# Retention followed by a token and channel mixer on one core: two loads of q moved to the hardware queue, a third batch in seven products, and a new order of work

## The chip, the cores and the metric

The kernel runs on one core of a Trainium2 chip. The time is the device time of one execution in microseconds (us). Before the change three runs gave 189.17, 189.81 and 190.44 us; their median is 189.81 us. One more execution was profiled, and the profile below is of that one.

The engines are named as in the profile: PE multiplies matrices, PEld loads its weights, DVE and ACT work elementwise, POOL (GpSimd) issues most of the loads here, and SP issues the stores, the transposes by DMA and one load. PSUM has eight banks, and a product lands in a bank before DVE or ACT takes it out.

## What is computed

Four batches, 8 heads, 768 tokens, 64 columns a head; x has 512 columns. The decay per head is a constant, so the kernel does the recurrence in six chunks of 128 tokens.

```python
state = gamma * state + k_t v_t^T               # per head, token by token
y_t   = (q_t state) / sqrt(64)                  # x = y, heads side by side: 4 x 768 x 512
h = relu(xT @ w_tok1) @ w_tok2                  # over tokens: 768 -> 256 -> 768
u = x + hT
out = u + relu(u @ w_ch1) @ w_ch2               # over channels: 512 -> 1536 -> 512
```

## The kernel before

**Tiling.** The work of a batch is cut in two. `front(b, p)` does the retention and the token mixing for one of four pairs of heads (128 columns): decay of k and q (L522, `decayed`), transposes of k and q by PE or by DMA (L538, `turn`), the states (L584, L596), the scores (L635) and their mask on DVE (`am`, L646), the rows of y (L666, L692), the two token products (L723, L743), and the evacuations to `x`, `u` and `X` (L708). At its end `uT`, the transposed u, is made for the pair. `back(b)` does the channel mixing of a batch: a wide product u @ w_ch1 to 1536 columns and a narrow one back to 512. Fronts of later batches run beside the backs of earlier ones.

**Two forms of the wide product.** `widen(sh)` is the direct one: for each half of the tokens and each of 12 column blocks four matmuls of 128x384 are summed in a bank (L822), and ACT takes it out with a relu (L838). `widen7()` is a product of 2x2 blocks in seven products instead of eight: four differences of `uT` on DVE (L861), then for each of six blocks seven products of two matmuls (L891), three copies of a bank kept aside (`us`, L902, ACT or DVE), three adds of bank and copy on DVE (L911), three relus on DVE (L915), and one relu straight out of a bank (L942 or L944). The combined weights that it needs are made on DVE once (L1138, tile `late`). A kept copy stands between two products in the same bank: the next product into that bank waits for it. Before the change `WIDE7` names batches 2 and 3. All four batches use the seven products in the narrow product (`narrow7`: L1005, L1041, L1051, L1031, L1058), except one part of batch 3, which is direct (`narrow`: L967, L976).

**What sets the order.** Nothing is scheduled at run time. `ORDERED` is a table of numbers of operations in the order in which they are issued, and `WAYS` picks for each the engine where two can do it. `arrange` walks the table with assumed durations and with `Rings`, a model of the DMA queues, and settles buffers and banks; the instructions are then issued in that order. Each engine works off its own list in order. Where the plan leaves PE idle in the first 21 us, matmuls on zeros are put in (L1164, tile `zero`).

**Loads.** They are issued by POOL with a cast from f32 to f16 on the way, in the order of `ORDER` as `ORDERED` places them. Only the first k (`HARD`) is loaded by SP as f32 into a buffer `us`; its decay makes f16 of it. q of batches 0 and 1 is loaded "wide": each partition takes six adjacent tokens, one run of 1536 bytes a head instead of 256. Its decay is multiplied in when the transposed q leaves its bank (L562, with the tile `late`).

Of the kernel before, what the change touches and what calls it, by code (L numbers as in the profile page):

```python
# [9 lines left out]
FP = mybir.dt.float32  # L10
# [28 lines left out]
class Rings:  # L39
# [5 lines left out]
    LAND = dict(SP=900, ACT=2000)  # L45
    DT = 40.0
    LATER = 1000
# [20 lines left out]
    def step(self, landed):  # L68
        dt, t = self.DT, self.t
        on = [(q, l[0]) for q, l in self.line.items() if l and l[0][2] <= t]  # L70
        if on:
            round_ = sum(x[0].dma[1] for _, x in on)
            for q, x in on:
                n = dt / round_
                if x[3] > t:
                    n = min(n, dt / self.GEN[q])
                x[1] -= n
                if x[1] <= 0:
                    self.line[q].pop(0)
                    landed.append((x[0], t + dt + self.land(q, x[0], t)))  # L80
        self.t = t + dt
# [9 lines left out]
def arrange(ops, BUFS, BANKS, seq, ways):  # L91
# [164 lines left out]

ORDERED = (
    "0b0d000a08050e0107020c2423040j060f292a030i2b250927260h282h2i2k0g332c2m342j0l352l37362d0k2e47382f2o2g0m43482q"
    "2n443h3i3k0n493l454a4b463m0q392p4c3a4h0o3j534d2r3b4k544e2s4i3c4f3d0p2t4j4g3e4l3f0s572u4m553g4n583n564o4p3p3o"
    "3q3r5i3s0u5l2v2y5m2w3t4r2x0v2z593u4q5a305h5b3v0t4s5c3y5d3w4t5e5j5f0w6763644u315k5g5o4v0r3z3x5n5p325q4w855r40"  # L260
    "0x4y4x86415s654z5t420z6650515u6894520y5v955y5w69115z6h5x76606j61hm1362hj6lij6ahn6k12hkim7372hp6b6ihlik106chq"
    "hsil6d77hrht74hois6e75786fithu79in7a147g7bioi4iu7jj16g7c6n7ihvhw7h6mj27ki5177d6oi77ei6iy6q1zhyhx6pi86rja21j3"
    "jgjh7f18206si9jijb6ti11c8182iv6ujciz6v6xig226yidi26w15hzi3iwi0jdihix83ia84ibj41aj01viej5iiip6z1w70j616j7icje"
    "if1yjn711987jj7m7o88iqjljo7lj81gjkir7nkb89j91xjfjp9z1b8ajukc7pjqaxjs8b1e7q8cjv8fk5jt8djy8i908gjw91k77r8hjxa0"
    "kgjm7s8ja18ek1khb0b18k7tjz8mk28l7u8njr7w1fb2k0a57x96kr8okk1d7v97ksk98pkl7y1h9892a6kaa28q93k61ukv99a78ra87z9a"
    "kwa9kea3809ba4aa8sk89cl0ay8tkt9eazkf9d8v9gkil19f8wkx9i8x9h8u9jl4kjctku9l9kky9m9n1ib3kdkn9ob4abb58ycu1sb69p8z"
    "b7kol21jb89qbvl5byadackz1ml39rag9u9sl9ae1t9vafl69wah9t9xl7bb9yaiajbfakal1nldbcamlelaanmdbdljbzmempc0mfaolfb9"
    "maapcvlkban4mqbeaqmrn5arcwbhm1bwbjasatbxllbgbiaumy1kmbn6kqavczc1mc1om2bkc2m7c3mzd0bldrmjepn0m8c4d1m3mkl8bmm9"
    "mlcxd2lyeq1lcybnmvkmlzlg1rd3bolbc5d4mwawbpbrmxlhbqm4k4dsm5k3bsc6mglibtlvm0lsd5m6c9eslmcdlwfnmhcblxlnlpcalolq"
    "ccltlrc7d7lummc8d8msd6mtcfdbmnn1etmod9njeumuminankn7ndcedtn2da1pn8nbnen9cgo5duncnfn3ddcidfcholevcjdxo6ordydv"  # L270
    "dzckdwe0glosnhewfoexe1noerclningdcnmey1qnpe2decmomnncpdgnlopcnezdhf0nqgmcqoonscrcsconrondie3ntoqfpnvf1djf2e5"
    "nwbuoufqe4e6dke8ovdnlce9dloynye7dmkpf3donzozowotdqdpf7eaebo1edeco3oxeef6p0eff4frf5ftegnuf9fup3o0nxeho4fso2f8"
    "faeip4o8p7ejp6p1fcfbgro7ekoafvo9fwfdgsocp9gtelfxodobfegup2ohffp8gooegvemoifgfyeneoofpbfhgwfjogpcpsfzfig1ptpg"
    "g4fkpdg5pxphpipepypjg2pzpkq0papufmplq1pqg0qqq2pngxpvgnq7q4flpoq9q8q5qgqrqxg3qaqvgyprqsqwqeqbqtqfqygpr7qcqzqh"
    "gqg6r0g8qir5gag7r2qjokr6g9ror3gbqlr9r8qmrercr1rppfqorardrqqdojrtpmr4rfqururrgcrgq3rwrhrvrxrmripwgdrjryqps3rn"
    "rbgerss4rzghqks0rkgfthtdgitjgjtfgktis1gggztesvh1tmh2srtoh0sws9tntph3h4tqqnssh6h5rlh7h8stt0q6h9tkt2t1tltrtss2"
    "tghattpptvtuhbt4s5hcs6t5hfhdt3sxs7hgt6s8sahihhsehet7sysbp5susgsfszsiscsht9t8sjsksdtbtzsnslsmu3uku0u4u5ulsoum"
    "u1u8upunu9uau6uqurubu2ustaucviutv8uduiuoufuuuzuguwv1vjuxvktwvnv2uvv3tyuevovlv6spvpv4v7vqtxv0vzvrv9wnvsvavxuj"
    "v5w1vbvuvywgvvvdvgvmw0vew6vhytw4w2whylwiu7w5w3wlvcuhymwjw7wmy5uyw8vwwowky6w9wpwevtwbwqwfwvvfsqwswrwcxnwwwtx1"
    "wdwuwaynxpxjxkyoxox3wxypxsxlx2wyyqxuxtxqxmxwx4x6wzxxxvx8x7xyx9yrydx0xaxzxcy0xby7x5y3y8xdysxfxetcy1xgxhy9xiy2"  # L280
    "yaxryey4yfybygyhyiycyuyvywyjyxyyykyzz0"
)
WAYS = (
    "000000000000000000000000000000000000000000000000000000000000000000000000000100000000000010000000000000100001"
    "001000000000000000000000000000000001101000000000000000000000000100100000100000000000000000000000000000000100"
    "001100000000000100000000000000011000001000000000001000000000000000000000010000000000000000000000000000000000"
    "000000000000000000000000000000000010001100000000000000000000010100000010010000000010000000000001001001011011"
    "000000010000000000100100100001100100000001100000000000000000000110110000000000000000000000000000010011000000"
    "010000000000000000100001001000000000000000000000000000000010010000000010000000000000000000000000000000000000"
    "000000000000000000000000000000000000000000000000000000000000000000000000000100000000000000000000011000000000"  # L290
    "000000000001100000000000000000000000000000000000000000000000000000000000000000000000000000000000000000000110"
    "000000000000000000001000000000000000000001100000000000000000000000000000000000000000000000000000000000001000"
    "000000000000000000000000000000000000000000000000000100000000010000000000000000000000100000000000000000000110"
    "000000000000000000000000000000000000000000000000000000000000000100000000000000000000000000000000000000000000"
    "0000000100000000011000000000000000000001000000001000000010000000100000001"
# [4 lines left out]
def kernel(  # L300
# [36 lines left out]
    WIDE7 = (2, 3,)  # L337
# [11 lines left out]
    HARD = {(0, 0, "k")}  # L349
# [129 lines left out]
    def load(b, p, what):  # L479
# [12 lines left out]
        dma = (96, 17) if hard else (16, 66) if wide else (96, 13.5)  # L492
# [6 lines left out]
    def front(b, p):  # L499
# [22 lines left out]
        def decayed(tag, src, dep, g, hard):  # L522
# [12 lines left out]
            return dst, got  # L535
        K, kl = decayed("k16", KF, kd, gk, (b, p, "k") in HARD)

# [200 lines left out]
        for j in range(2):  # L738
# [12 lines left out]
            t2 = op(one("PE", (335, 500), emit), [hr, wops["t2"], x_ops[j]], [], [H1, Y[j]])  # L751
# [50 lines left out]
    def back(b):  # L802
# [150 lines left out]
        def narrow(sh, blocks=range(HC)):  # L953
            H2, rel = H2s[sh], rels[sh]
            for i in blocks:
# [3 lines left out]
                for cols in cuts:  # L959
# [23 lines left out]
                    op(either(emit, ACT=(380, 101), SP=(450, 100)), [ad], [], [X], dma=(8, 90 * w_ // C))  # L983


        def narrow7(i0, i1):
# [95 lines left out]
            for i, d in ((i1, [o21, o22]), (i0, [o11, o12])):  # L1082
                def emit(e, i=i):
                    (nc.sync if e == "SP" else nc.scalar).dma_start(out=out[b, i * P:(i + 1) * P, :], in_=X.tile[:, i])
                op(either(emit, ACT=(380, 101), SP=(450, 100)), d, [], [X], dma=(8, 90))
# [111 lines left out]
```

## Time and profile before

| | before |
|---|---|
| median of three runs | 189.81 us |
| the profiled execution: time | 190.01 us |
| the profiled execution: span of its instructions | 188.2 us |
| granted PE clock | 0.999 |
| instructions: PE, DVE, ACT, POOL | 2109, 448, 282, 62 |
| moved by DMA | 24.92 MB |

Times inside the profile count from the start of the span; 1.8 us of the time lie outside it. A busy share is the union of an engine's instructions over the span. "x192 | 36.0, 326" in a group means 192 instructions with 36.0 us of busy time in all and 326 ns for one; where the instructions overlap, 36.0 / 192 is the smaller number and is what one costs in a row of many. The chain of waits follows the end of the program back, step by step, to what released each instruction.

### The profile page before, as it was taken

How to read it: one execution, taken by the hardware profiler on the slowest of the kernel's cores; microseconds unless marked ns; L12 is line 12 of the kernel's file. 1: busy time of each engine (PE TensorE's matmuls, PEld its weight loads, DVE VectorE, ACT ScalarE, POOL GpSimd, SP SyncE). 2: the span in 40 equal slices, each digit the busy share in tenths (PEclk: the TensorE clock that was granted, in tenths of full speed). 3: DMA queues.
4: the chain of work that ended last, by engine and by line, in shares of the span. 5: the costliest groups of instructions: out<-in, count | busy, mean ns of one | idle time of the engine just before them, and what ended most of it. 6: DMA issues, size and time to landing. Idle time of an engine off the chain costs nothing.

```text
span 188.2 us, 5284 instructions
## 1 busy us (share of the span) xinstructions
PE 181.2 (96%) x2109; PEld 136.7 (73%) x2109; DVE 166.5 (88%) x448; ACT 124.2 (66%) x282; POOL 52.8 (28%) x62
## 2 busy tenths in 40 slices
PE   7989999999999999999999899999999999999993
PEld 3455888667688988776668788965678986567872
DVE  3789999997889999958799989999999999999982
ACT  3965989569889898478663686598883444575100
POOL 7995686536440708405202200000000000000000
PEclk9999999999999999999999999999999999999999
DMA  9999999999999999999999979724312031121045
GB/s 122 155 157 196 179 188 177 208 191 201 159 155 144 125 155 122 147 136 163 195 163 127 115 99 251 158 43 86 98 56 45 0 101 56 72 98 59 0 177 215
DMA packets 91977, 24.92 MB, mean 132 GB/s; under 512 B 81968, under 2 KB 89008, under 8 KB 91952
## 3 DMA queue, kind: packets, MB, share of 16 engines
q0 software_dynamic: 67456, 13.18, 85.3%
q1 hardware_dynamic: 23776, 10.10, 24.5%
q10 hardware_dynamic: 720, 1.31, 1.9%
q8 instruction: 16, 0.26, 0.6%
q14 instruction: 9, 0.07, 0.1%
HBM read 26.74 MB, written 6.29 MB: 175 GB/s over the span
## 4 chain that ended last, share of the span: by engine, by line
PE 78%; DVE 12%; DMA 3%; ACT 2%; issue 2%; POOL 1%; SPq 0%; POOLq 0%; ACTq 0%; DVEq 0%
PE bank L822 16%; PE bank L891 15%; PE bank L1041 14%; PE bank L1051 10%; PE bank L743 5%; DVE am L646 4%; PE bank L723 4%; PE bank L635 3%; PE bank L967 3%; DMA kT<-k 3%; DVE U L596 2%; PE bank L666 2%; PE bank L692 2%; DVE qT L562 2%; PE bank L584 1%
## 5 line engine op out<-in xcount | busy, mean ns | idle before, releaser
L822 PE MATMUL bank<-uT,wc 128*128 128x384 f16 x192 | 36.0, 326 | 0.0
L646 DVE TENSOR_TENSOR am<-bank,mask 128x384 f16<-128x384 f32 x64 | 33.2, 549 | 1.7 <-PE bank L635 1.5
L838 ACT ACTIVATE h<-bank 128x384 f16<-128x384 f32 x48 | 21.5, 500 | 10.3 <-PE bank L822 10.3
L490 POOL DMA_DIRECT2D v<-in_v_dram x16 | 16.4, 1031 | 40.0 <-PE bank L692 17.9
L822 PEld LDWEIGHTS <-wc 128*128 128x128 f16 x192 | 17.2, 98 | 9.1 <-DVE X L708 0.2
L902 ACT COPY us<-bank 128x384 f32<-128x384 f32 x34 | 15.5, 481 | 8.9 <-PE bank L891 6.4
L1041 PEld LDWEIGHTS <-hs 128*128 128x128 f16 x198 | 18.5, 98 | 3.0 <-issue 0.7
L1031 ACT COPY us<-bank 128x256 f32<-128x256 f32 x31 | 11.8, 384 | 13.3 <-PE bank L1041 13.0
L911 DVE TENSOR_TENSOR h<-bank,us 128x384 f16<-128x384 f32 x36 | 19.3, 553 | 1.1 <-PE bank L891 0.4
L1058 DVE TENSOR_TENSOR X<-X,bank 128x256 f32<-128x256 f32 x44 | 17.9, 414 | 2.2 <-PE bank L1051 1.4
L1041 PE MATMUL bank<-wsum,hs 128*128 128x256 f16 x132 | 17.9, 273 | 0.6 <-ACT us L1031 0.6
L596 DVE SCALAR_TENSOR_TENSOR U<-U,gp,bank 128x64 f32<-128x64 f32 x64 | 17.1, 281 | 0.7
L708 ACT CAST x<-bank 128x384 f16<-128x384 f32 x30 | 14.1, 492 | 5.0 <-PE bank L692 5.0
L490 POOL DMA_DIRECT2D k<-in_k_dram x15 | 15.4, 1035 | 5.3 <-DVE U L596 1.7
L708 ACT CAST u<-bank 128x384 f16<-128x384 f32 x28 | 13.2, 489 | 3.4 <-PE bank L743 3.2
L891 PE MATMUL bank<-hs,late 128*128 128x384 f16 x72 | 14.9, 326 | 0.0
L743 PE MATMUL bank<-h,wt 128*128 128x128 f16 x192 | 14.7, 219 | 0.0
L891 PEld LDWEIGHTS <-late 128*128 128x128 f16 x96 | 9.0, 98 | 6.4 <-issue 0.4
L1051 PEld LDWEIGHTS <-h 128*128 128x128 f16 x132 | 12.5, 98 | 1.6
L614 ACT ACTIVATE cross<-U,gp 64x320 f16<-64x320 f32 x23 | 12.8, 560 | 1.2 <-DVE U L596 0.7
L723 PE MATMUL bank<-x,wt 128*128 128x128 f16 x192 | 13.3, 219 | 0.0
L743 PEld LDWEIGHTS <-wt 128*128 128x128 f16 x192 | 11.9, 98 | 1.6
(89 smaller groups left out, 374.2 us busy)
## 6 DMA issues: line engine op xcount, KB each, us to landing
out_dram<-X SPq DMA_DIRECT2D x18, 256.0 KB, 2.4
v<-in_v_dram POOLq DMA_DIRECT2D x16, 192.0 KB, 6.7
q<-in_q_dram POOLq DMA_DIRECT2D x16, 192.0 KB, 7.3
k<-in_k_dram POOLq DMA_DIRECT2D x15, 192.0 KB, 7.2
wc<-in_moe_w_ch_dram POOLq DMA_DIRECT2D x5, 512.0 KB, 13.4
out_dram<-X ACTq DMA_DIRECT2D x5, 256.0 KB, 2.1
wt<-in_moe_w_tok_dram POOLq DMA_DIRECT2D x2, 384.0 KB, 9.1
wc<-in_moe_w_ch_dram POOLq DMA_DIRECT2D x2, 256.0 KB, 9.0
```

The costliest lines, as they stand in the source:

```text
L490: (nc.sync if hard else nc.gpsimd).dma_start(out=tile_of(s, [P, 2, NC, D], FP if hard else F16), in_=src.rearrange("h (c p) d -> p (h c) d ...
L596: nc.vector.scalar_tensor_tensor(out=u[:, c], in0=u[:, c - 1], scalar=gp[:, p:p + 1], in1=st, op0=ALU.mult, op1=ALU.add)
L646: nc.vector.tensor_tensor(am, SC[g].tile[:, :m * P].rearrange("p (i t) -> p i t", t=P), mask.to_broadcast([P, m, P]), ALU.mult)
L708: (nc.scalar.copy if e == "ACT" else nc.vector.tensor_copy)(tile(), t)
L723: nc.tensor.matmul(acc[:, jt * P:(jt + 1) * P], wt1[:, i, jt * P:(jt + 1) * P], X16.tile[:, i].rearrange("p h d -> p (h d)"), start=(i == ...
L743: nc.tensor.matmul(Y[j].tile[:, 2 * i * D:2 * (i + 1) * D], wt2[:, jt, t], H1.tile[:, jt], start=False, stop=(jt == NJ - 1), skip_group_ch ...
L822: nc.tensor.matmul(acc[:, :SH], wc1[:, ct, ft * P:(ft + 1) * P], UT.tile[:, ct, sh * SH:(sh + 1) * SH], start=(ct == 0), stop=(ct == NP - 1))
L838: nc.scalar.activation(H2.tile[:, ft], A.tile[:, :SH], AF.Relu)
L891: nc.tensor.matmul(acc[:, :SH], left(ct), r[:, ct], start=first and ct == 0, stop=ct == C2 - 1, skip_group_check=True)
L911: nc.vector.tensor_tensor(h(m, sh), R.tile[:, :SH], KS.tile[:, j], ALU.add)
L1041: nc.tensor.matmul(acc_[:, lo], l[:, j], r[:, j], start=first and j == 0, stop=j == K2 - 1, skip_group_check=True)
L1051: nc.tensor.matmul(acc_[:, lo], l[:, j], r[:, j], start=first and j == 0, stop=j == K2 - 1, skip_group_check=True)
```

## The change

1. q of the first two pairs of batch 0 is loaded by SP's hardware queue, as f32 and wide, into buffers `hs`; one new copy for each (ACT or DVE) makes f16 of it. k of the first pair, on the same queue, now stands behind the two in SP's list.
2. `WIDE7` takes batch 1 too, so three of four wide products are made of seven products.
3. The weights of the second token product are loaded in two halves.
4. The constants of the DMA model are others, the digits of the table have base 62, and `ORDERED` and `WAYS` are new throughout.

```diff
-    LAND = dict(SP=900, ACT=2000)
+    LAND = dict(SP=900, ACT=900)
     DT = 40.0
-    LATER = 1000
+    SOFT = 0.6
+    LATER = 700
...
-            return 1470 if t < 6000 else 2900 if t < 13500 else 2300
+            return 1470 if t < 4500 else 2100 if t < 17000 else 1700 if t < 30000 else 2000
...
-            round_ = sum(x[0].dma[1] for _, x in on)
+            hard = len(on) - ("POOL" in dict(on))
             for q, x in on:
-                n = dt / round_
+                share = (self.SOFT if hard else 1.0) if q == "POOL" else (1.0 - self.SOFT if hard < len(on) else 1.0) / hard
+                n = share * dt / x[0].dma[1]
...
 ORDERED = (
-    "0b0d000a08050e0107020c2423040j060f292a030i2b250927260h282h2i2k0g332c2m342j0l352l37362d0k2e47382f2o2g0m43482q"
...
+    "0c0500040a0e090b070d010h03061e0f1j0j1P0g1k021U0i1g1f1Q1V1h1R0k1l1i081S1m1n1T1t1o0l1W1v1u1p251X1q1Y0m1r1x2q29"
...
-    WIDE7 = (2, 3,)
+    WIDE7 = (1, 2, 3,)
...
-    HARD = {(0, 0, "k")}
+    HARD = {(0, 0, "q"), (0, 0, "k"), (0, 1, "q")}
...
-        s = Slot("us" if hard else what)
+        s = Slot(("hs" if wide else "us") if hard else what)
...
-                nc.gpsimd.dma_start(out=tile_of(s, [P, 2, NC, D], F16).rearrange("p h c d -> p h (c d)"),
+                (nc.sync if hard else nc.gpsimd).dma_start(
+                                    out=tile_of(s, [P, 2, NC, D], FP if hard else F16).rearrange("p h c d -> p h (c d)"),
                                     in_=src.rearrange("h (p c) d -> p h (c d)", c=NC))
...
+        if (b, p, "q") in HARD:
+            QH, QF = QF, Slot("q")
+
+            def emit(e):
+                d = tile_of(QF, [P, 2, NC, D], F16)
+                (nc.scalar.copy if e == "ACT" else nc.vector.tensor_copy)(d, QH.tile)
+            qd = op(either(emit, ACT=act(S, 0, 1), DVE=dve(S, 0.54)), [qd], [QF], [QH])
...
-            t2 = op(one("PE", (335, 500), emit), [hr, wops["t2"], x_ops[j]], [], [H1, Y[j]])
+            t2 = op(one("PE", (335, 500), emit), [hr, wops["t2" + "ab"[j]], x_ops[j]], [], [H1, Y[j]])
...
-        elif what == "t2":
-            weight("t2", 16, 150, wt2, moe_w_tok2)
+        elif what[:2] == "t2":
+            half = slice(0, SH) if what == "t2a" else slice(SH, S)
+            weight(what, 16, 64, wt2[:, :, half], moe_w_tok2[:, half])
```

The lines of the changed kernel are 13 to 15 higher than those of the same code before (L562 is L575, L911 is L924). The order that the table makes is shown at three places.

**The first loads on POOL.** `in_q`, `in_k` and `in_v` are the inputs, `wt` the token weights, `away` and `us` tiles of constants that DVE and ACT need at the start. Before:

```order
L490 DMA v<-in_v_dram 128x12x64
L400 ISA
L400 IOTA away 128x128
L487 DMA q<-in_q_dram 128x2x384
L490 DMA k<-in_k_dram 128x12x64
L487 DMA q<-in_q_dram 128x2x384
L420 IOTA us 128x384
L487 DMA q<-in_q_dram 128x2x384
L490 DMA k<-in_k_dram 128x12x64
L490 DMA v<-in_v_dram 128x12x64 x2
```

After:

```order
L405 IOTA away 128x128
L425 IOTA us 128x384
L496 DMA k<-in_k_dram 128x12x64
L496 DMA v<-in_v_dram 128x12x64 x2
L496 DMA k<-in_k_dram 128x12x64
L492 DMA q<-in_q_dram 128x2x384
L496 DMA k<-in_k_dram 128x12x64
L496 DMA v<-in_v_dram 128x12x64
L492 DMA q<-in_q_dram 128x2x384
L475 DMA wt_79<-in_moe_w_tok_dram 128x6x256
```

The constants are made first, the two q are gone from this list, and k and v of the second and third pair move up. On SP the two q now stand ahead of the first k.

**DVE at the first scores.** `U` are the states, `bank_N` a bank of PSUM, `hs` the f32 q. Before:

```order
L530 TENSOR_SCALAR k_125<-us,gk 128x6x64
L594 COPY U<-bank_154 128x64
L416 TENSOR_SCALAR ident_73<-away 128x128
L596 TENSOR_SCALAR U<-U,gp,bank_154 128x64
L447 MEMSET cross_76 128x320
L447 MEMSET cross_77 128x320
L447 MEMSET cross_78 128x320
L562 TENSOR_TENSOR qT<-bank_184,late 128x768
L646 TENSOR_TENSOR am<-bank_209,mask 128x384
```

After:

```order
L421 TENSOR_SCALAR ident_73<-away 128x128
L547 COPY q<-hs 128x768
L575 TENSOR_TENSOR qT<-bank_151,late 128x768
L536 TENSOR_SCALAR k_196<-us,gk 128x6x64
L575 TENSOR_TENSOR qT<-bank_181,late 128x768
L447 TENSOR_SCALAR mask<-away 128x128
L607 COPY U<-bank_220 128x64
L609 TENSOR_SCALAR U<-U,gp,bank_220 128x64 x2
L659 TENSOR_TENSOR am<-bank_246,mask 128x384
```

The transposed q of two pairs now comes ahead of the first decayed k and of the states; two qT stand in front of the first `am` where one stood.

**DVE at the end of the program.** `X` is the output tile, `us` a kept copy, `hs` a sum of h. Before:

```order
L1058 TENSOR_TENSOR X<-X,bank_3499 128x256
L1058 TENSOR_TENSOR X<-X,us 128x512
L1058 TENSOR_TENSOR X<-X,bank_3424 128x256
L1058 TENSOR_TENSOR X<-X,bank_3415 128x256
L1058 TENSOR_TENSOR X<-X,us 128x256
L976 TENSOR_TENSOR X<-X,bank_3387 128x512
L976 TENSOR_TENSOR X<-X,bank_3515 128x256
L976 TENSOR_TENSOR X<-X,bank_3360 128x128
```

After:

```order
L1071 TENSOR_TENSOR X<-X,bank_3522 128x256
L989 TENSOR_TENSOR X<-X,bank_3505 128x128
L1071 TENSOR_TENSOR X<-X,us 128x512
L1071 TENSOR_TENSOR X<-X,bank_3587 128x256
L1071 TENSOR_TENSOR X<-X,bank_3438 128x256
L1071 TENSOR_TENSOR X<-X,us 128x256
L1071 TENSOR_TENSOR X<-X,bank_3605 128x256
L1071 TENSOR_TENSOR X<-X,us 128x256
L1071 TENSOR_TENSOR X<-X,bank_3456 128x256
```

The direct product of batch 3 stood last and left small pieces (128x256, 128x128) to store; now the last two groups of seven products stand last, and whole rows of 128x512 are stored after them.

More of the change, by code (lines that the diff above doesn't have):

```diff
@@ L262 @@
[L262 to L271, printed above, removed]
@@ L296 @@
+    "000000000000000000000000000000000000000000000000000000110000000000000000000011000000010000000100000000000000"
+    "00"
 )
@@ L491, in emit @@
                                                            in_=src.rearrange("h (c p) d -> p (h c) d", p=P))
-        dma = (96, 17) if hard else (16, 66) if wide else (96, 13.5)
+        dma = (16, 64) if hard and wide else (96, 17) if hard else (16, 66) if wide else (96, 13.5)
         if hard:
@@ L1102 @@
     for what in ORDER:
-        n = int(what[1])
+        n = int(what[1:2])
         if what[0] in "kqv":
@@ L1145 @@
         back(b)
-    seq = [int(ORDERED[2 * i:2 * i + 2], 36) for i in range(len(ORDERED) // 2)]
+    digit = {c: i for i, c in enumerate(DIGITS)}
+    seq = [digit[a] * 62 + digit[c] for a, c in zip(ORDERED[::2], ORDERED[1::2])]
     asked = set(o.n for o in queue)
```

67 lines of the change are left out of this document (39 added, 28 removed).

## The prediction

> **What bounds the kernel now.** I read the shares first, then a table by stage, then the chain of waits, then the groups by line. Part 1 of the page:
>
> ```profile
> PE 181.2 (96%) x2109; PEld 136.7 (73%) x2109; DVE 166.5 (88%) x448; ACT 124.2 (66%) x282; POOL 52.8 (28%) x62
> ```
>
> PE leads and DVE is close behind. By stages (start:end in us, then the length, then busy time and count of PE, PEld, DVE, ACT and POOL, granted clock, DMA share, GB/s). The cuts are the first wide product at 33.2, the narrow one of batch 0 from about 54, the wide product of batch 1 from 78.4, its narrow one from 97.6, and the wide products of batch 2 (125.0) and batch 3 (156.6):
>
> ```profile
> core 0: us, PE busy (x) PEld busy (x) DVE busy (x) ACT busy (x) POOL busy (x), PEclk, DMA share, GB/s
> 0.00:33.20 33.20, 30.21 (x463) 21.67 (x464) 27.66 (x89) 24.97 (x49) 25.58 (x35) 1.00 1.69 168
> 33.20:54.00 20.80, 20.80 (x211) 13.88 (x209) 17.03 (x36) 15.24 (x34) 9.09 (x9) 1.00 1.74 186
> 54.00:78.40 24.40, 24.28 (x356) 21.21 (x352) 24.00 (x67) 20.79 (x48) 11.10 (x11) 1.00 2.07 140
> 78.40:97.60 19.20, 19.20 (x204) 12.85 (x202) 15.02 (x42) 13.62 (x32) 5.04 (x5) 1.00 1.54 173
> 97.60:125.00 27.40, 26.72 (x374) 22.79 (x372) 25.98 (x72) 18.23 (x47) 2.02 (x2) 1.00 0.83 133
> 125.00:140.30 15.30, 15.30 (x128) 9.89 (x123) 14.64 (x40) 12.66 (x32) 0.00 (x0) 1.00 0.33 81
> 140.30:156.60 16.30, 16.30 (x181) 14.55 (x180) 15.48 (x40) 6.81 (x19) 0.00 (x0) 1.00 0.20 53
> 156.60:188.20 31.60, 28.34 (x217) 19.87 (x214) 26.64 (x69) 11.92 (x28) 0.00 (x0) 1.00 0.26 95
> ```
>
> From 33.2 on PE has no gap except 0.7 us between 97.6 and 125. But DVE is busy for about 95% or more of every stage from 54 to 156.6, save the wide product of batch 1 (15.02 of 19.20), and that is the one that the change makes dearer for DVE. Is PE's 96% real, with matmuls that overlap? The chain tells (start, length, what):
>
> ```profile
> 17.07 0.47 DVE am L646
> ...
> 33.41 3.58 PE bank L822 x22
> ...
> 98.80 5.15 DMA kT<-k
> ...
> 125.13 7.75 PE bank L891 x46
> ...
> 182.43 2.53 PE bank L967 x24
> ```
>
> 22 matmuls of 128x384 take 3.58 us, 163 ns each, and 46 of the seven-product form 7.75 us, 168 ns each. They follow without a gap, so a matmul less there is 165 ns less. Before 33 us the chain runs mostly through DVE (`am` back to back at 0.47), so the start is bound otherwise.
>
> **The change part by part.** The sum is made against the profiled execution, 190.0 us (span 188.2 and 1.8 around it), which lies 0.2 above the median of 189.81; within 1% of that median is about what a measurement here can't tell from no change.
>
> *Seven products in batch 1, on PE.* The direct form has 2 halves x 12 blocks x 4 = 96 matmuls; the other 6 blocks x 7 x 2 = 84. Twelve fewer at 165 ns: **-2.0 us**, all of it in a stage where PE has no gap. I take it whole if DVE and ACT keep up.
>
> *The same, on DVE and ACT.* Prices from the groups by line (busy time over count is what one costs in a row):
>
> ```profile
> L646 DVE TENSOR_TENSOR am<-bank,mask 128x384 f16<-128x384 f32 x64 | 33.2, 549 | 1.7 <-PE bank L635 1.5
> L911 DVE TENSOR_TENSOR h<-bank,us 128x384 f16<-128x384 f32 x36 | 19.3, 553 | 1.1 <-PE bank L891 0.4 <-ACT us L902 0.2
> ...
> L915 DVE TENSOR_SCALAR h<-h 128x384 f16<-128x384 f16 x36 | 7.6, 251 | 0.0
> ...
> L616 DVE TENSOR_SCALAR cross<-U,gp 64x320 f16<-64x320 f32 x9 | 4.8, 539 | 0.2
> L530 DVE TENSOR_SCALAR k<-k,gk 128x384 f16<-128x384 f16 x13 | 4.7, 369 | 0.0
> ...
> L708 DVE COPY X<-bank 128x384 f32<-128x384 f32 x8 | 4.4, 551 | 0.6 <-ACT u L708 0.6
> ```
>
> DVE gains 18 adds at 0.54 (9.7), 18 relus at 0.21 (3.8), 4 differences, a kept copy, a kT copy and a relu from a bank, each taken like L708's 0.55 (3.9), and one cast of q. That cast of 768 columns isn't in the trace; between 0.55 (one copy) and 1.1 (two of them) I take 0.8. It hands over 14 decays at 0.36 (5.0), 3 `cross` at 0.53 (1.6), 6 copies at 0.55 (3.3) and 3 relus of 256 columns, at two thirds of a copy (1.1). Sum +18.2 - 11.0 = +7.2, so DVE goes to some 173.7 us. ACT:
>
> ```profile
> L838 ACT ACTIVATE h<-bank 128x384 f16<-128x384 f32 x48 | 21.5, 500 | 10.3 <-PE bank L822 10.3
> L902 ACT COPY us<-bank 128x384 f32<-128x384 f32 x34 | 15.5, 481 | 8.9 <-PE bank L891 6.4 <-DVE h L911 2.5
> ...
> L708 ACT COPY X<-bank 128x384 f32<-128x384 f32 x24 | 11.7, 504 | 0.1
> L528 ACT ACTIVATE k<-k,gk 128x384 f16<-128x384 f16 x17 | 10.0, 613 | 2.5 <-DMA kT<-k 2.2
> ```
>
> ACT loses 24 relus at 0.45 (10.8) and gains 17 kept copies at 0.46 (7.8), 5 relus at 0.45 (2.3), 14 decays at 0.59 (8.3), 12 other evacuations, `cross` and relus net, at 0.48 (5.8), and a cast in place of a kT copy: +13.4, to 137.6. Neither engine is full over the whole span. But both are slacker only before 54 us and between 78 and 98, so a little is lost where PE meets an answer late. Bounds: 0, if the order hides all, and +2.0, the whole gain of PE. Nearest are the stages of batch 2 and 3, where the seven products run with DVE at 95% and PE without a gap; I take **+0.8**. The queue behind a late kept copy is PE's own: the next product into the same bank, and all matmuls behind it.
>
> *The start.* Loads and scores:
>
> ```profile
> out_dram<-X SPq DMA_DIRECT2D x18, 256.0 KB, 2.4
> ...
> us<-in_k_dram SPq DMA_DIRECT2D x1, 384.0 KB, 3.8
> ...
> out_dram<-X SPq DMA_DIRECT2D x2, 64.0 KB, 1.8
> ```
>
> ```profile
> 9.44 0.51 PE L635 MATMUL bank<-qT,kT 64*128 64x128 f16 x12 [0.20 <-DVE qT L562]
> ```
>
> The first scores at 9.44 us wait for qT on DVE. Now two q as f32, 384 KB each like k, come ahead of k on SP. k took 3.8 us alone; with twice its bytes ahead it may land 2 to 4 us later, but two qT and the casts are to be done meanwhile. POOL starts its loads two constants later and has two loads fewer. Up to the third uT copy on DVE the order has two qT and one `am` fewer and two of the small relus fewer, one `cross` and a cast more: some 2.2 us less DVE work ahead of the first wide product, which starts at 33.2 now. Bounds: -2.2, if DVE alone counts, and +1.0, if the first scores come later by what k loses beyond the work in between. I take the middle of the lower part, **-1.2**. The casts cost nothing themselves as long as qT's wait hides them; uncovered they are 0.8 us, once. The halves of the token weights add one issue on POOL and let the first half of the second token product start earlier; POOL has 7.6 us free in the first 33 and the issue is hidden.
>
> A rule speaks against this part. POOL is busy 25.58 of the first 33.2 us with 35 instructions, 0.73 each, and the DMA engines show a share of 1.69. The Trainium skill (DMA: Bandwidth & Descriptors, "Issuing engines are not separate DMA queues") says that DMAs started from several engines run on the same 16 DMA engines and interleave, so that starting them elsewhere saves the issue time alone. The busy DMA share in that row agrees with it. By the rule only the two issues of POOL are gained; that case is the third rival.
>
> *A stall in the old order.* In the chain at 98.80 a transpose by DMA ends last for 5.15 us, and PE loses 0.7 us in that stage. The new order puts all those transposes anew; the stall goes or comes back elsewhere (-0.7 to +0.7): **-0.5**.
>
> *The end.* The direct matmuls of batch 3 that filled PE for its last 2.53 us, waiting for nobody, now stand earlier; the last products need copies and sums, and after the last add a store of 256 KB (2.4 us to landing) stands where 64 KB (1.8) stood. Bounds 0 and +1.2 (the 0.6 twice, since two rows end together): **+0.5**.
>
> Sum: -2.0 + 0.8 - 1.2 - 0.5 + 0.5 = -2.4; 190.0 - 2.4 = **187.6 us**, own range 186.2 to 188.9.
>
> **The rivals.**
>
> *1. DVE becomes the bound from batch 1's narrow product on (slower).* After 97.6 DVE now does 25.98 + 14.64 + 15.48 + 26.64 = 82.7 us. In the new order that part holds 7 more `am`, 5 more adds and 6 more relus, 4 fewer decays, and little else: 7 x 0.52 + 5 x 0.54 + 6 x 0.21 - 4 x 0.36 - 0.7 = +5.5, so 88.2. My forecast leaves it 185.8 (span) - 2.9 (issue and store) - 96.4 (97.6 less 1.2) = 86.5. If DVE is never idle there, `am` costs 0.47 as in the chain instead of 0.52; with such a saving on 65 masks and adds 88.2 shrinks to 84.9 and just fits. If not, at the share of the stage from 54.0 (24.00 of 24.40) it needs 89.6 and the time is 96.4 + 89.6 + 2.9 + 1.8 = 190.7; at 95%, as in 140.3 to 156.6, 193.9. Middle 192.3. It decides from 86.5 us on. For it: DVE is at about 95% there already. Against: those stages ran so with PE full. 0.22, of which 0.02 under 191.7.
>
> *2. ACT delays the wide product of batch 1.* From batch 0's last relu to batch 1's last kept copy the order gives ACT 91 instructions, at 0.46 some 42 us, beside about 43 us of PE; now ACT's fullest stage is 20.79 of 24.40, 85%. At 92% it needs 45.7, 1.8 more than the forecast allows: 189.4. 0.13.
>
> *3. The start gains only issue time.* Then the -1.2 falls away, since POOL isn't what the first product waits for: 188.8. For it the 1.69 above, against it the shorter list of DVE. 0.10.
>
> *4. The start gains more.* If data of the second and third pair come earlier as well as DVE having less to do, the first wide product starts 3.0 us earlier, not 1.2: 185.8. Against it: PE has fillers and gaps of only a few us there to lose. 0.12.
>
> **How the numbers follow.** The forecast has 0.43: 0.26 under 187.9 and 0.17 above. Faster by over 1%: 0.26 + 0.12 = 0.38. Within 1%: 0.17 + 0.13 + 0.10 + 0.02 = 0.42. Slower: 0.20. The range goes from the fourth rival to the middle of the first, 185.5 to 192.1, and leaves out some 0.15.
>
> **What would show it.** PE: 12 fewer matmuls and no gap over 0.3 us between first and second wide product, the first at 32 us or earlier (start). DVE: some 173 busy us, and after batch 1's narrow product idle time left (against rival 1); if DVE shows 98% to the end and PE rows wait for `X` or `am`, rival 1 holds. ACT: kept copies in batch 1 that begin at once after their product (against rival 2). The last store about 3 us after the last matmul. The prediction is wrong if PE's non-filler work isn't 2 us less, or if its gaps grow by more than 3 us.

## The result, and the profile after

The changed kernel took 190.76 us (median of five runs, 190.27 to 191.39); the kernel before, run beside it, 189.29 us (189.17 to 190.44). The ratio is 1.0075, with a 95% interval of 1.0059 to 1.0091: slower by 1.4 us, where 2.4 us less was forecast. The profiled execution took 190.65 us, with a span of 188.9. The profiled execution of before (190.01) lay 0.7 above the median that its kernel now shows, so the two profiles differ by only 0.66 us of span.

Part 1 of the page after:

```profile
PE 180.1 (95%) x2096; PEld 135.6 (72%) x2096; DVE 171.2 (91%) x466; ACT 135.7 (72%) x306; POOL 52.3 (28%) x61
```

PE has 13 matmuls fewer (12 of the wide product and one filler on zeros), DVE 4.7 us more, ACT 11.5 us more. By stages, cut at the same steps as before (start:end in us, length, busy time and count of PE, PEld, DVE, ACT and POOL, granted clock, DMA share, GB/s):

```profile
0.00:32.80 32.80, 29.57 (x436) 20.80 (x437) 26.37 (x88) 25.23 (x51) 24.41 (x34) 1.00 1.73 179
32.80:56.00 23.20, 23.20 (x245) 15.88 (x243) 20.90 (x44) 16.52 (x37) 10.56 (x11) 1.00 1.78 184
56.00:80.00 24.00, 22.58 (x340) 19.71 (x338) 21.96 (x60) 22.03 (x51) 9.55 (x10) 1.00 1.84 130
80.00:100.00 20.00, 19.93 (x213) 13.24 (x212) 19.81 (x60) 19.30 (x46) 6.73 (x7) 1.00 1.70 170
100.00:126.50 26.50, 26.24 (x348) 22.05 (x346) 26.37 (x71) 22.44 (x55) 1.01 (x1) 1.00 0.68 101
126.50:141.50 15.00, 15.00 (x160) 10.15 (x159) 14.28 (x41) 12.53 (x31) 0.00 (x0) 1.00 0.33 75
141.50:157.50 16.00, 16.00 (x157) 14.25 (x156) 15.74 (x43) 5.53 (x15) 0.00 (x0) 1.00 0.51 104
157.50:188.90 31.40, 27.54 (x213) 19.52 (x210) 25.80 (x68) 12.13 (x28) 0.00 (x0) 0.97 0.27 102
```

The stall that stood between 97.6 and 125 is gone (0.26 us of PE's idle time are left between 100 and 126.5), and a bigger one stands between 56 and 80 (22.58 of 24.00). In batch 1's wide product, 80 to 100, DVE and ACT are now both full: 19.81 and 19.30 of 20. The groups that changed most:

```profile
L659 DVE TENSOR_TENSOR am<-bank,mask 128x384 f16<-128x384 f32 x64 | 32.6, 547 | 1.3 <-PE bank L648 1.2
L924 DVE TENSOR_TENSOR h<-bank,us 128x384 f16<-128x384 f32 x54 | 28.9, 550 | 1.1 <-PE bank L904 0.6
L915 ACT COPY us<-bank 128x384 f32<-128x384 f32 x51 | 24.0, 485 | 7.7 <-PE bank L904 4.4
```

The adds went from 36 to 54 and the copies kept on ACT from 34 to 51, at the prices of before.

A busy PE is no measure of its work, since matmuls overlap in the records and fillers count. So I added up every matmul of both traces that isn't a filler at its number of columns, 160 ns for 384 of them (a little under the 163 of the chain); what is left of PE's time is lost. Cut to the terms of the prediction, in us of the two profiled executions (batch 1's wide product runs from 78.4 to 97.6 us before and from 80 to 100 after):

| | before | after | difference | forecast |
|---|---|---|---|---|
| products (all that isn't filler) | 166.57 | 164.60 | -1.97 | -2.0 |
| PE lost or on fillers, 0 to 50 us (the start) | 13.62 | 14.34 | +0.72 | -1.2 |
| PE lost, 50 to 110 us outside batch 1's wide product (the stalls) | 2.35 | 2.83 | +0.48 | -0.5 |
| PE lost in batch 1's wide product | 0.25 | 1.08 | +0.83 | +0.8 |
| PE lost, 110 us to the last matmul | 1.93 | 1.92 | 0 | 0 |
| start of the last matmul to the end of the span | 3.49 | 4.10 | +0.61 | +0.5 |
| sum: the span | 188.21 | 188.87 | +0.66 | -2.4 |

Three terms came out as forecast. Two didn't: the start, by 1.9 us, and the stall, by 1.0. These are two single executions; for the start that matters, as shown next.

**The start.** Scores and what they wait for, on PE, ACT and DVE of the kernel after (start, length, what, and in brackets the idle time and what ended it):

```profile
12.44 0.34 PE L648 MATMUL bank<-qT,kT 64*128 64x128 f16 x6 [0.17 <-ACT kT L580]
```

```profile
3.87 1.28 ACT L438 ACT_TABLE_LOAD   x1 [3.87 <-DVE lnsc L412]
5.17 2.50 ACT L438 ACTIVATE late<-us,lnsc,lnh 128x384 f32<-128x384 f32 x4
7.58 0.82 ACT L547 CAST q<-hs 128x768 f16<-128x768 f32 x1
8.30 0.20 ACT L417 ACTIVATE gk<-lgs 128x8 f32<-128x8 f32 x1
8.60 0.60 ACT L534 ACTIVATE k<-us,gk 128x384 f16<-128x384 f32 x1
```

The first scores come 3 us later than before (9.44). They need the transposed k, that needs k's decay (8.60), and that needs `gk`, which ACT makes at 8.30, behind a table load that waits until 3.87, the constants `late` and a cast.

One of these 3 us is PE's own pace in this execution. Seven matmuls on zeros behind q's first transposes, here and then in run 2 below, whose order is the same up to there:

```profile
6.84 2.42 PE L1179 MATMUL bank<-zero 128*128 128x384 f16 x7
```

```profile
6.51 1.31 PE L1179 MATMUL bank<-zero 128*128 128x384 f16 x7
```

The column of the granted clock shows 1.00 for both, but the trace's record of that clock begins, at full, only at 9.76 us here and at 4.52 in run 2. Ahead of that time the zeros start 0.32 us apart, behind it 0.16. All that follows comes 1.0 us earlier in run 2: the first scores at 11.44, the first wide product at 31.84 instead of 32.83. So the start has to be compared over several executions. The runs are told below; up to 50 us runs 2, 3, 5 and 6 have the loads and the order of the changed kernel (all in us):

| profiled execution | full clock from | first scores | first wide product | PE lost up to 50 |
|---|---|---|---|---|
| before | 7.08 | 9.44 | 33.25 | 13.62 |
| run 8 (order of before) | 5.04 | 9.30 | 33.14 | 13.50 |
| after | 9.76 | 12.44 | 32.83 | 14.34 |
| run 2 | 4.52 | 11.44 | 31.84 | 13.38 |
| run 3 | 5.00 | 11.44 | 32.43 | 13.95 |
| run 5 | 9.94 | 12.51 | 32.91 | 14.42 |
| run 6 | 10.28 | 12.69 | 33.09 | 14.58 |
| run 4 (q by POOL) | 4.95 | 10.83 | 31.94 | 13.47 |
| run 7 (q by POOL) | 4.48 | 11.01 | 32.14 | 13.67 |

With the clock full by 5 us the changed start loses 13.4 to 14.0 us, as much as before; with the late clock 14.3 to 14.6. Executions whose PE begins with eleven zeros, idle from about 4.8 to 6.1 us, had the late clock in three of six; those that begin with fourteen or more had it full at 7.08 at the latest, in eight of eight. That the shorter row of zeros is the reason isn't shown.

The loads say more. Queues and issues of the first 13 us, before and then after (queue: packets, MB, share; load: count, KB each, us to landing):

```profile
q0 software_dynamic: 7823, 1.48, 139.9%
q1 hardware_dynamic: 1552, 0.39, 13.4%
...
us<-in_k_dram SPq DMA_DIRECT2D x1, 384.0 KB, 3.8
```

```profile
q0 software_dynamic: 7219, 1.08, 123.7%
q1 hardware_dynamic: 2096, 1.18, 34.9%
...
hs<-in_q_dram SPq DMA_DIRECT2D x2, 384.0 KB, 3.7
...
us<-in_k_dram SPq DMA_DIRECT2D x1, 384.0 KB, 6.0
```

POOL's queue brings f16 (2 bytes a value), SP's f32 (4). Before, 1.48/2 + 0.39/4 = 0.84 million values come in by 13 us; after, 1.08/2 + 1.18/4 = 0.84 million. More bytes move, but no more values: the second queue changes only which come first, and k of the first pair now lands 6.0 us after its issue, behind two q.

**The stall.** The chain of waits after, and PE's row:

```profile
63.45 5.77 DMA kT<-k
...
69.33 0.61 ACT k L534
...
70.91 0.38 ACT us L1044
```

```profile
71.34 0.81 PE L1054 MATMUL bank<-wsum,hs 128*128 128x256 f16 x6 [1.42 <-ACT us L1044]
```

A decay of k on ACT waits until a transposing DMA has read an older decayed k, since it needs that buffer (`k16`, three of them). Behind it in ACT's list stands a kept copy, and PE's next product waits for that.

### The profile page after: what moved, and what is told of

It reads as the page before. It is cut to its first block, busy times and chain, and to the rows that moved or that the text cites. A ratio compares the mean times of both kernels' runs of the same rounds, so it can differ in the third digit from the quotient of the medians.

```text
span 188.9 us, 5318 instructions
## 1 busy us (share of the span) xinstructions
PE 180.1 (95%) x2096; PEld 135.6 (72%) x2096; DVE 171.2 (91%) x466; ACT 135.7 (72%) x306; POOL 52.3 (28%) x61
## 4 chain that ended last, share of the span: by engine, by line
PE 72%; DVE 11%; ACT 8%; DMA 5%; issue 1%; SPq 0%; DVEq 0%; ACTq 0%
PE bank L904 18%; PE bank L1054 13%; PE bank L1064 9%; PE bank L835 8%; PE bank L756 4%; PE bank L736 4%; DVE h L924 3%; DMA kT<-k 3%; PE bank L980 3%; PE bank L648 3%; ACT k L534 3%; DMA hs<-in_q_dram 2%; PE bank L679 2%; PE bank L1179 2%; PE bank L565 2%; DVE am L659 2%
## 5 line engine op out<-in xcount | busy, mean ns | idle before, releaser
L924 DVE TENSOR_TENSOR h<-bank,us 128x384 f16<-128x384 f32 x54 | 28.9, 550 | 1.1 <-PE bank L904 0.6
L915 ACT COPY us<-bank 128x384 f32<-128x384 f32 x51 | 24.0, 485 | 7.7 <-PE bank L904 4.4
L904 PE MATMUL bank<-hs,late 128*128 128x384 f16 x108 | 22.3, 326 | 0.0
L904 PEld LDWEIGHTS <-late 128*128 128x128 f16 x144 | 13.4, 98 | 8.1 <-issue 0.2
L835 PE MATMUL bank<-uT,wc 128*128 128x384 f16 x96 | 17.4, 326 | 0.0
L904 PE MATMUL bank<-uT,wc 128*128 128x384 f16 x72 | 16.4, 326 | 0.0
L627 ACT ACTIVATE cross<-U,gp 64x320 f16<-64x320 f32 x26 | 14.6, 560 | 1.4 <-DVE U L609 0.8
L534 ACT ACTIVATE k<-k,gk 128x384 f16<-128x384 f16 x24 | 14.2, 614 | 1.6 <-DMA kT<-k 1.5
L851 ACT ACTIVATE h<-bank 128x384 f16<-128x384 f32 x24 | 11.0, 495 | 5.6 <-PE bank L835 5.3
L721 ACT COPY X<-bank 128x384 f32<-128x384 f32 x29 | 14.1, 499 | 0.0
L904 PEld LDWEIGHTS <-wc 128*128 128x128 f16 x108 | 9.8, 98 | 5.8 <-issue 0.5
```

The costliest lines, as they stand in the source:

```text
L534: nc.scalar.activation(t, src.tile[:, j], AF.Copy, scale=g[:, h:h + 1])
L721: (nc.scalar.copy if e == "ACT" else nc.vector.tensor_copy)(tile(), t)
L835: nc.tensor.matmul(acc[:, :SH], wc1[:, ct, ft * P:(ft + 1) * P], UT.tile[:, ct, sh * SH:(sh + 1) * SH], start=(ct == 0), stop=(ct == NP - 1))
L904: nc.tensor.matmul(acc[:, :SH], left(ct), r[:, ct], start=first and ct == 0, stop=ct == C2 - 1, skip_group_check=True)
L915: (nc.scalar.copy if e == "ACT" else nc.vector.tensor_copy)(ks[:, j], R1.tile[:, :SH])
L924: nc.vector.tensor_tensor(h(m, sh), R.tile[:, :SH], KS.tile[:, j], ALU.add)
```

## The experiments

Times are medians, the ratio is to the kernel before run beside them, with its 95% interval. The runs of before that stood beside the three larger groups had medians of 189.33, 189.58 and 189.52 us.

**1. The activation's table loaded early** (`table_early`), in the changed kernel, by an exponential that is not otherwise needed:

```diff
     nc.vector.memset(zero, 0.0)
+    warm = const_p.tile([P, 1], FP, name="warm")
+    nc.scalar.activation(warm, zero[:, :1], AF.Exp)
```

> The changed kernel with one exponential on a column of zeros as ACT's first instruction, so that the table load (1.28 us) no longer stands behind the wait for DVE at 3.87 us. Theory A (the start is bound by ACT's chain table load, late, cast, gk, k): the first scores come 1.2 to 1.5 us earlier than 12.44 us, and the time falls from 190.76 by 0.6 to 1.2 us. Theory B (the start is bound by the loads, or the 33 us to the first wide product are filled by DVE anyway): the first scores come earlier too, but the first wide product stays at 33.0 and the time within 0.3 us.

190.67 us, ratio 1.0054 (1.0027 to 1.0082). In the profile the table load moves from 3.87 to 0.73, and the next thing is late at once:

```profile
0.73 1.28 ACT L1172 ACT_TABLE_LOAD   x1 [0.73 <-PEq L1198]
...
8.45 0.62 ACT L534 ACTIVATE k<-us,gk 128x384 f16<-128x384 f32 x1 [1.04 <-DMA us<-in_k_dram]
```

`gk` is ready at 7.22, but k lands at 8.4. Two waits lay on top of each other. The first scores come at 11.02 us, 0.4 earlier than in run 2, whose clock was full as early (4.57 and 4.52 us); PE loses 13.51 us up to 50, no less than there (13.38), and the interval shows no gain either.

**2. Four buffers for the decayed k** (`k16_four`); the order of all engines stays:

```diff
-    BUFS = dict(late=1, k=4, q=4, v=4, k16=3,
+    BUFS = dict(late=1, k=4, q=4, v=4, k16=4,
```

> The changed kernel with four buffers for the decayed k instead of three, and nothing else. Theory A (ACT, held at 63 to 69 us by a k buffer that a transpose by DMA still reads, holds PE's 1.6 us gap at 69.6): the gap goes, the time falls by 1.0 to 1.6 us. Theory B (the transposes themselves are late, since the DMA engines are full there): ACT goes on, but the scores that need that transposed k wait in its place; the time falls by under 0.4 us.

190.30 us, ratio 1.0037 (1.0012 to 1.0062). The gap at 70 is gone, so the buffer was its cause. But a gap of 1.05 us stands ahead of 75.45, where scores wait for a transposed k. Most of the gain went to the next wait.

**3. Batch 1's wide product direct again** (`b1_direct`), in the new order, its matmuls and relus in the places of the seven products:

```diff
-    WIDE7 = (1, 2, 3,)
+    WIDE7 = (2, 3,)
```

> The changed kernel with the direct wide product in batch 1, its matmuls and relus put where the seven products stood; all else in the new order. PE has 12 matmuls more (2.0 us), DVE 40 instructions fewer (some 16 us). Theory A (the seven products gain, less what PE waits in that stage, 1.2 us): slower than 190.76 by 0.5 to 1.0 us. Theory B (DVE became the bound and the seven products of batch 1 are a loss): faster by 0.5 to 1.5 us, and DVE shows idle time after 80 us.

193.50 us, ratio 1.0220 (1.0189 to 1.0251): 2.7 us slower than the changed kernel. DVE sinks to 82%, and it doesn't help; between 80 and 100 us PE loses 1.87 us, where the changed kernel's loses 1.08:

```profile
PE 180.1 (94%) x2108; PEld 136.0 (71%) x2108; DVE 157.6 (82%) x426; ACT 136.3 (71%) x306; POOL 52.2 (27%) x61
```

The seven products themselves are a gain, of the size of their twelve matmuls (2.0) or somewhat more; the order was made for them, so 2.7 may flatter them. That DVE had become so full that the seven products of batch 1 are a loss is refuted. The first rival is about the part behind that product, which this run leaves as it is.

**4. q of the first two pairs by POOL again** (`q_by_pool`), with the cast on the way, no copies, the rest of the order as changed:

```diff
-    HARD = {(0, 0, "q"), (0, 0, "k"), (0, 1, "q")}
+    HARD = {(0, 0, "k")}
```

> The changed kernel with q of the first two pairs loaded by POOL with the cast on the way again, at the head of POOL's list (first and third), without the two copies; all else in the new order. Theory A (the hardware queue gains nothing: q was at 5.27 us and had to be copied for 0.7 us, POOL's first load would land near 6): first transposes of q at about 6.3 instead of 6.05, the time within 0.4 us of 190.76. Theory B (the two loads relieve POOL's queue, and k and v of the later pairs come later without it): slower by 0.8 to 1.5 us.

190.36 us, ratio 1.0039 (1.0019 to 1.0059). First scores at 10.83 instead of 12.44. By the medians, taking the hardware queue away from q gains some 0.4 us in the new order (the intervals of the two ratios just touch). The traces don't show it in the loads: with the clock full by 5 us, PE loses 13.47 us up to 50 here, and 13.38 in run 2 with q on SP. POOL's q comes with fourteen zeros at the start instead of eleven, so the gain may be the clock's; one profiled execution each can't tell. The hardware queue had gained nothing either way.

**5. The old end** (`tail_old`): the steps of batch 3's `back` in their relative order and on the engines of before; only `ORDERED` and `WAYS` differ.

> The changed kernel with the steps of batch 3's channel mixing in the relative order (and on the engines) that they had before; all else as changed. Theory A (the end costs what the last products' copies and sums and the larger last stores take, +0.4 to +0.7): 190.1 to 190.3 us against 190.7, and the last DVE instruction ends about 0.5 us after the last matmul's start with the last store landing 2.9 us after it, as before. Theory B (the end is neutral, the loss lies ahead of it): 190.6 to 190.9. If the old end fits badly into the new slots, PE shows gaps after 155 us and the time is above 191.

190.89 us, ratio 1.0071 (1.0047 to 1.0095): no gain. From the last matmul to the end of the span it takes 3.7 us, between the 3.5 of before and the 4.1 after. But between 50 and 110 us, where the order is the changed one, PE loses 4.44 us here and 3.91 after: executions differ there by more than the 0.4 in question. The end's cost in the table above stands as a reading of the trace; this run doesn't turn it into time.

**6. Less for DVE in batch 1's wide product** (`no_relu1`); its 18 relus on DVE are left out, and with them that part of the computation:

```diff
-                        nc.vector.tensor_scalar(h(m, sh), h(m, sh), 0.0, None, ALU.max)
+                        if b != 1:
+                            nc.vector.tensor_scalar(h(m, sh), h(m, sh), 0.0, None, ALU.max)
```

> The changed kernel without the 18 relus that DVE does in place in batch 1's wide product (L928, 0.21 us each in a row, 3.8 us of DVE in all); that part of the computation is left out, all else is as changed. Theory A (in the wide product of batch 1 DVE is what ends last, and the 1.05 us that PE loses between 90 and 100 us come from it): that idle time falls under 0.3 us and the time to about 189.7. Theory B (PE waits there for kept copies on ACT or for banks, whatever DVE does): the idle time stays near 1 us and the time within 0.3 us of 190.7.

189.89 us, ratio 1.0015 (0.9995 to 1.0036): 0.9 us less than the changed kernel. The windows of 90 to 100 us, after and then this run:

```profile
90.00:100.00 10.00, 9.93 (x106) 6.37 (x105) 9.89 (x30) 9.35 (x23) 3.18 (x4) 1.00 1.74 146
```

```profile
90.00:100.00 10.00, 10.00 (x109) 6.58 (x107) 8.49 (x20) 9.54 (x24) 3.57 (x4) 1.00 1.82 163
```

By the sum of matmuls PE's loss from 90 to 101 us falls from 1.07 to 0.36 us. The wait that ends the stage in the changed kernel, for an add on DVE, is gone:

```profile
100.45 0.81 PE L1054 MATMUL bank<-wc,h 128*128 128x256 f16 x6 [0.26 <-DVE h L924]
```

So DVE is last in that stage (9.89 of 10), though ACT is nearly as full.

**7. POOL's q and four buffers together** (`pool_k16`): the edits of 2 and 4.

> The changed kernel with q of the first two pairs loaded by POOL again (with the cast on the way, no copies) and with four buffers for the decayed k instead of three. Singly these gave 190.36 and 190.3 us against 190.7. Theory A (two separate losses, start and stall): both gains add, 189.9 to 190.0 us, with the stall at 69 us gone and the first scores at 11 us or earlier. Theory B (the gain of one is lost at the next wait, the scores' wait for the transposed k at 74 us): 190.2 to 190.4 with a gap of 1 us or more there.

189.67 us, ratio 1.0016 (0.9996 to 1.0036). By the medians the two gains add, to 1.1 us of the changed kernel's 1.4. The buffer's part is seen in the trace (the gap at 70 is gone), the start's isn't (13.67 us lost up to 50, in run 2 13.38). What remains can't be told from zero, and a gap remains to be had:

```profile
76.01 0.51 PE L646 MATMUL bank<-qT,kT 64*128 64x128 f16 x12 [1.30 <-DMA kT<-k]
```

**8. Four buffers in the kernel before** (`before_k16`), the same edit as in 2; only banks are numbered otherwise.

> The kernel before with four buffers for the decayed k instead of three; same order, only banks are numbered otherwise. If the stall at 104.7 us of the kernel before (0.77 us) came from a late buffer like the one at 69 us of the changed kernel: it goes, and the time is 188.5 to 188.8 against 189.3. If it came from the transposing DMA itself: it stays, and the time is within 0.3 us of 189.3. In both cases it is a second look at the start of the kernel before: first scores between 9 and 10 us, PE's idle and filler time before 30 us some 12 us.

188.99 us, ratio 0.9971 (0.9954 to 0.9988). From 98 to 108 us, before and then this run:

```profile
98.00:108.00 10.00, 9.32 (x124) 7.80 (x123) 9.65 (x29) 5.31 (x14) 2.02 (x2) 1.00 1.04 111
```

```profile
98.00:108.00 10.00, 9.93 (x135) 8.52 (x133) 9.89 (x30) 6.17 (x16) 2.03 (x2) 1.00 1.07 115
```

The old stall had the same cause, one buffer too few, and goes with the fourth. This is the only version that beats both kernels, by 0.3%. The first scores come at 9.3 us here too.

**9 and 10. The transposes of batch 2's second pair earlier** (`early_kt`), **and two loads of batch 3 put behind three of batch 2 as well** (`both_moves`), both from run 7, in the table alone.

> The version with q by POOL and four buffers for the decayed k (189.67 us; PE loses 1.5 us at 74.5 where the scores wait for a transposed k), with the four steps ahead of that transpose moved forward in the table: two decays of batch 2's second pair, and its two transposes on SP, k ahead of q. Theory A (the transposes are issued too late, the lane itself is quick enough): the transposed k lands 2 to 3 us earlier, the gap at 74 falls under 0.4 us, the time is 188.4 to 188.8. Theory B (the DMA engines are full there, and each of the transposes in a row takes its 3 to 5 us whenever it is issued): the gap stays above 0.8 us or appears at the next transpose, and the time is 189.3 to 189.9.

> The same with two loads of batch 3 (k and q of its first pair) put behind three loads of batch 2 in POOL's list, so that they don't run beside those transposes. Theory A: like the run before or 0.2 us better, 188.3 to 188.8. Theory B: only this run removes the gap (188.4), the one before doesn't; or, if loads are always under way there whatever their order, neither does.

190.67 us (ratio 1.0061, 1.0035 to 1.0087) and 190.14 us (1.0034, 1.0014 to 1.0054): neither better than run 7 (1.0016). Run 9 lies above both ranges that were expected of it, and why it is 1.0 us slower than run 7 is open. The gap stays, at 75, and now the q ends it, since k went ahead; from the chains of waits of the two runs:

```profile
66.39 9.96 DMA qT<-q
```

```profile
66.13 10.27 DMA qT<-q
```

In run 10 the four transposes of the two pairs are issued from 61.8 to 66.1 us, and the last has landed at 76.4, where run 7 had it at 76.0: 14.6 us or 3.6 each. It is their row that takes so long, with POOL's loads under way beside them; neither moving the transposes nor moving two loads helped. That the loads are the reason isn't shown.

**11. k ahead of q on SP, with the early table** (`k_first`), in the changed kernel.

> The changed kernel with the table of the activation loaded early and k ahead of the two q on SP's queue. Theory A (the first scores are late because the table load stood behind a DVE wait and k stood behind two q): k lands at about 5.3 us, its decays are done by 8.5, the first scores start at 10 us or earlier, and the time is 0.5 to 0.9 us under the 190.7 of the changed kernel. Theory B (the queue's share among 1.1 MB of loads decides, and whichever comes last holds the scores): then the second q lands at 8.5 and its cast and transposes hold the pair behind, the first scores come at 11 us, and the time is 190.3 to 190.7.

190.71 us, ratio 1.0072 (1.0044 to 1.0099): nothing gained. Issues of the first 13 us:

```profile
hs<-in_q_dram SPq DMA_DIRECT2D x2, 384.0 KB, 5.1
...
us<-in_k_dram SPq DMA_DIRECT2D x1, 384.0 KB, 3.6
```

k lands in 3.6 us, and each q in 5.1 instead of 3.7. The scores (12.27) now stand behind q's transposes, which start at 8.81 instead of 6.05. Whichever comes last holds the pair.

**12. The loads alone, in the kernel before** (`before_hardq`), in its order, with a copy for each q and ten more matmuls on zeros in the start:

```diff
-    HARD = {(0, 0, "k")}
+    HARD = {(0, 0, "q"), (0, 0, "k"), (0, 1, "q")}
...
+        if (b, p, "q") in HARD:
+            QH, QF = QF, Slot("q")
+
+            def emit(e):
+                d = tile_of(QF, [P, 2, NC, D], F16)
+                (nc.scalar.copy if e == "ACT" else nc.vector.tensor_copy)(d, QH.tile)
+            qd = op(either(emit, ACT=act(S, 0, 1), DVE=dve(S, 0.54)), [qd], [QF], [QH])
```

> The kernel before, in its own order, with only the loads of the change: q of the first two pairs of batch 0 as f32 on SP's queue ahead of the first k, and a copy that makes f16 of each (first on DVE, second on ACT), put right ahead of its transposes; ten more matmuls on zeros stand in PE's start by the plan. Theory A (these loads themselves bring the first scores later, since k and the copies stand behind 768 KB more on one queue): first scores at 11 to 12 us instead of 9.4, PE's idle and filler time before 30 us up by 1 us or more, the time 190.2 to 191.2 against 189.5. Theory B (the loads are neutral; it is the new order of the start that is later): first scores within 0.7 us of 9.4 and the time 189.3 to 189.8. The prediction's reading (they gain): 188.9 or less.

193.41 us, ratio 1.0226 (1.0184 to 1.0268): 3.8 us slower than the 189.62 of before, far beyond both theories. PE loses 17.37 us up to 50 (13.62 before), with the clock full from 6.44. The chain of waits at its start:

```profile
1.76 6.61 DMA us<-in_k_dram
...
8.46 0.61 ACT k L530
9.07 2.39 ACT late L434 x4
...
12.14 1.03 ACT k L530 x2
...
13.21 0.36 PE bank L644 x6
```

k lands at 8.4 instead of 4.5. In the old lists k's decay stands ahead of the constants `late` on ACT and of `ident` and `cross` on DVE, so all of these slip with it. The first wide product starts at 37.1 instead of 33.3. The new order puts `late` and q's transposes ahead of k and so earns this back: 13.4 to 14.0 us are lost there with the early clock. The two edits of the start belong together: the order mends what the loads cost, and no gain is left.

## Why the prediction was wrong

The time lies in the widest range given (185.5 to 192.1) and within 1% of before, but above the forecast's own range (186.2 to 188.9), and the sign was wrong: -2.4 was forecast, +1.4 was measured.

**The failed step: "The start", with its -1.2.** No profiled execution shows that gain. With the clock full by 5 us the changed start lost 13.38 and 13.95 us against 13.62 and 13.50 with the order of before, so between -0.2 and +0.5; with the late clock it lost 14.34 to 14.58, +0.7 to +1.1. The step had two errors. First, "some 2.2 us less DVE work ahead of the first wide product, which starts at 33.2 now" was read as a gain. The first wide product did come earlier, at 32.83 (31.84 in run 2), but with less done: 20.0 us of products stood ahead of it before, 18.35 after. Those 1.65 us weren't saved but moved behind it, where PE is full. PE's loss ahead of the first wide product went from 13.25 us (33.25 - 20.0) to 14.48 (32.83 - 18.35), and with the early clock of run 2 to 13.50: in neither did it fall. What counts is the time that PE loses, not when a chosen product starts. Second, "k ... may land 2 to 4 us later, but two qT and the casts are to be done meanwhile" had the delay right (4.5 to 7.8) and took the cover for a gain: run 12 shows at 3.8 us how much stands behind k, and the new order covers that and no more. The bound of +1.0 held the +0.72; the value taken inside the bounds didn't. Beyond these two, the sum took PE's pace for given, and the late clock, worth 1.0 us (14.34 against 13.38), stands in no term. If the median of the changed kernel is such an execution too, this is most of the 1.4; only the profiled ones show their clock.

The third rival gave the start no gain, and for this term it was right: 0.84 million values in 13 us by either way, and with the early clock no less lost by PE. The Trainium skill ("DMA: Bandwidth & Descriptors", "Issuing engines are not separate DMA queues") says that DMAs started from several engines share the same 16 DMA engines, so that starting them elsewhere saves issue time only. The 0.84 million agree with that. The rival missed that the order of arrival can cost (run 12).

**"A stall in the old order", -0.5.** "The stall goes or comes back elsewhere" is what happened, but larger: PE lost 1.03 us from 104 to 106 before and 1.74 from 68 to 72 after, +0.7, the upper bound; the row of the table, with all else in it, has +0.48. Its cause, three buffers for the decayed k, could have been read: the chain showed a transposing DMA ending last, and the diff left `BUFS` alone. A stall whose cause a change doesn't touch isn't to be counted as gone.

**Right.** *Seven products on PE*: -1.97 for -2.0, and run 3 confirms the gain. *The same on DVE and ACT*: +0.83 in that stage for +0.8, or +1.3 with the wait at 100.45 that ends it and that the table counts with the stalls; run 6 shows DVE as what ends last there. DVE's busy time was 171.2 for 173.7, ACT's 135.7 for 137.6. *The end*: +0.61 for +0.5 in the trace. *The first rival*: PE lost nothing more after 110 us (1.92 for 1.93), with DVE at 15.74 of 16.00 there. *The second rival* was half right: ACT is at 19.30 of 20 in batch 1's wide product, but what run 6 takes from DVE is what PE gains.

**The baseline.** The sum started from an execution that was 0.7 us above its kernel's median; the difference of the two profiles (0.66) and that of the medians (1.5) differ mostly by this. No run here shows where that execution lost it.

**Open.** Why the new order isn't faster even with four buffers and the early clock. The profiled executions of runs 2 and 8 have both, and took 189.01 and 188.88 us (run 2's is the fastest of its twelve, whose median is 190.30). In run 2 the products are 1.9 us less and the start 0.1, but PE loses 1.8 us more between 50 and 110, about 1 each in the gap at 75 and in batch 1's wide product, and the end takes 0.6 more. Only DVE's part was tried singly with a result. Open too is what makes the clock late, and in how many of the other executions it was.

## What to carry to other kernels

Count a start by the time that the bound engine loses in it, not by when one product begins: work that has left the stretch may only have moved. Compare the pace of equal matmuls first: where it differs, a single execution says little about the order. A load on another queue brought no more data here; ask what it pushes back, and what stands behind that in each engine's list. And where a stall moves under a new order, look for the buffer that it waits for: here one more buffer, an edit of one digit, did more than the whole change.

## What the runs showed of the hardware

- Matmuls of 384 columns on zeros started 0.32 us apart until the record of the granted clock began and 0.16 apart behind it, while the column of that clock showed 1.00 for both. With one and the same order the record began at 4.52 us in one execution and at 9.76 in another, and the start lost 1.0 us more in the latter.
- A table load of ACT stood where the wait of the next activation was: it ran at 3.87 us where that activation waited for DVE, and at 0.73 us ahead of one that didn't, 1.28 us long both times.
- A copy of 768 columns from f32 to f16 took 0.70 us on DVE and 0.82 on ACT in the changed kernel, and on DVE 0.50 in run 12 and 1.15 in run 11.
- Four transposing DMAs issued in a row, with loads under way, took some 3.6 us each (run 10: the last landed 14.6 us after the first was issued), and the last 10.3 us from its own issue.
